# A decode block with a 537 MB key-value cache: 8 MB tiles of 64 KB rows in three slots, K turned in place, scores read in PSUM, 512-wide matmuls, output weights last

## The chip, the core and the metric

The program runs on one core of one Trainium2 chip. The metric is the device time of one execution in microseconds. The median of three executions is 1338.72 us (1338.3 to 1338.79).

## The reference

Two tokens (B = 2 sequences, one position each) pass through one block in float32. The row x (512 wide) is normalized, projected to 32 query heads of 128, and attends to a cache of 8 key-value heads with 32,768 positions each; four query heads share a key-value head. The attention output goes through wo (4096 x 512), and is multiplied by silu of a small gated network of the same x (512 to 1792 to 512).

```python
xn = layernorm(x)
q = (xn @ wq).reshape(2, 1, 32, 128).transpose(0, 2, 1, 3)
scores = einsum("bhqd,bhkd->bhqk", q, repeat(k_cache, 4)) * 128 ** -0.5
p = softmax(scores)
s = einsum("bhqk,bhkd->bhqd", p, repeat(v_cache, 4)).reshape(2, 1, 4096) @ wo
gate, up = xn @ W_gate, xn @ W_up
g = silu(((gate * (gate > 0)) * up) @ W_down)
return x + s * g
```

K and V are 268 MB each. With wq (8.39 MB), wo (8.39 MB), gate and up (7.34 MB) and down (3.67 MB) the core reads 564.67 MB once; nothing of it is used twice.

## The kernel before

**Tiles.** The work falls into 16 groups, one for each pair of sequence and key-value head, each with its 32,768 positions. A group's K and V come in eight tiles each of 4096 positions: 2 MB, in which each of 128 partitions holds 32 consecutive positions, one row of 16 KB. All large loads go through one queue, SP's (`load`, L118), into a ring of eight 16 KB slots per partition, which the weights share. A load is issued when the slot that it takes has been released by its last reader.

**Steps.** The main loop has one step per K tile. `k_transposes` turns the tile on DVE by 32 x 32 blocks, in two instructions of 2048 columns (L282), from its ring slot into one of two further buffers. `scores` (L293) multiplies the turned tile with the group's queries: 16 matmuls of 256 columns, four column groups of the array side by side, and four slices of the head dimension accumulated. One DVE instruction (L303) then scales the scores, copies them from PSUM to SBUF and keeps each row's maximum. When a group's eight tiles are through, `maximum` (L309 to L327) takes the group's maximum through PE and DVE to a negative bias. `weights` runs the exponential on ACT (L333), brings the weights into position with a matmul (L337) and turns them on DVE (L341). `values` multiplies them with a V tile: 32 matmuls of 128 columns in four column groups (L349). At a group's end `take_o` (L369) scales the output by the reciprocal of the sum, and `finish_group` (L377 to L401) brings it into columns. After the second sequence of a head it multiplies with that head's 1 MB of wo (L392) and adds to the sum.

**Order.** The values of a tile come nine steps (`OFF`) behind its scores: in step s the program does the transposes and scores of tile s, the weights of tile s - 8, and the values of tile s - 9. Thus one group's scores run among the values of the group ahead. Loads are written three steps (`DEPTH`) before their use. The gate, up and down weights and the heads' parts of wo are loaded between the K and V tiles. The last V tile comes in three pieces, and behind it the last head's part of wo.

In the trace each matmul of the program appears as two MATMUL and two LDWEIGHTS instructions: 128 tiles with 16 score matmuls give the 4096 of L293.

## Time and profile before

| | |
|---|---|
| median of three executions | 1338.72 us |
| profiled execution: span from first to last instruction | 1336.6 us |
| what the median has beyond that span | 2.1 us |
| busy: PE, DVE, ACT | 847.6, 731.2, 69.1 us |
| mean granted TensorE clock | 0.857 |
| bytes of queue 1 (all loads of SP) | 564.68 MB in 40,776 packets |
| read from HBM | 564.67 MB, 422 GB/s over the span |

Of the profiled execution the profile gives the span alone, and no time of its own. A row of a stage table has the stage, its length, then the busy time and number of instructions of PE, PE's weight loads, DVE, ACT and POOL, then the granted PE clock (1.00 is full), the mean busy share of the 16 DMA engines, and GB/s. A share can pass 1.0 by a little, since packets of one engine overlap at their edges. A row of the groups has line, engine, operation, tiles, shapes and count, then busy us and the mean ns of one, then idle time before them and what ended it. A row of the timeline has start, length, engine, line and count; neighbouring instructions are merged, so its length is that of the whole run.

### The profile page before, as it was taken

What the parts mean: (1) busy time and instruction counts of PE and PEld (TensorE: products, weight loads), DVE (VectorE), ACT (ScalarE), POOL (GpSimd) and SP (SyncE); (2) the same over time, 40 slices, a digit from 0 to 9 for tenths busy, and PEclk for the clock granted to TensorE, in tenths of its full rate; (3) what the DMA queues carried; (4) which work ended last, traced back from release to release, by engine and by line L of the source; (5) the groups of instructions that cost most, each with busy time, mean ns of one, the idle gap of its engine ahead of it and who ended that gap; (6) DMA issues with size and microseconds to landing.
All of it is one profiled execution on the core that took longest, in us unless ns stands there. A gap on an engine that the chain in (4) does not pass through costs nothing.

```text
span 1336.6 us, 28791 instructions
## 1 busy us (share of the span) xinstructions
PE 847.6 (63%) x13288; PEld 487.1 (36%) x13288; DVE 731.2 (55%) x973; ACT 69.1 (5%) x261; POOL 1.3 (0%) x7
## 2 busy tenths in 40 slices
PE   4657666665666656666656666666666666666665
PEld 1333333433334333333434333333333433333343
DVE  5775555646556464555555555465554655556450
ACT  0001010100101010010100001010010100001010
POOL 0000000000000000000000000000000000000000
PEclk9787878978889897888988887898888988789899
DMA  9999999999999999999999999999999999999995
GB/s 397 431 430 430 429 430 429 430 428 430 429 431 428 429 429 430 430 429 428 430 429 430 430 430 430 428 427 431 430 430 430 428 429 428 431 430 424 430 429 246
DMA packets 40951, 566.52 MB, mean 424 GB/s; under 512 B 4462, under 2 KB 4478, under 8 KB 6784
## 3 DMA queue, kind: packets, MB, share of 16 engines
q1 hardware_dynamic: 40776, 564.68, 99.1%
q8 instruction: 104, 1.70, 0.5%
q14 instruction: 15, 0.12, 0.0%
q10 hardware_dynamic: 24, 0.01, 0.0%
q0 software_dynamic: 32, 0.00, 0.0%
HBM read 564.67 MB, written 0.00 MB: 422 GB/s over the span
## 4 chain that ended last, share of the span: by engine, by line
issue 100%; POOLq 0%; POOL 0%
POOLq L488 0%; POOL ident masks.py:199 0%; POOL ident masks.py:197 0%; POOLq masks.py:199 0%; POOLq L475 0%
## 5 line engine op out<-in xcount | busy, mean ns | idle before, releaser
L293 PE MATMUL s<-kts,qt 128*32 128x256 f32 x4096 | 464.7, 523 | 414.9 <-DVE kts L282 409.0
L282 DVE STREAM_TRANSPOSE kts<-k 128x2048 f32<-128x2048 f32 x256 | 573.2, 2277 | 4.2 <-DMA k<-in_A_k_cache_dram 4.2
L293 PEld LDWEIGHTS s<-kts,qt 128*32 128x32 f32 x4096 | 178.1, 140 | 657.7 <-issue 344.8
L349 PE MATMUL o_ps<-v,pts 128*4 128x128 f32 x8192 | 352.4, 297 | 10.0 <-DMA v<-in_A_v_cache_dram 9.5
L349 PEld LDWEIGHTS o_ps<-v,pts 128*4 128x4 f32 x8192 | 260.3, 94 | 71.8 <-issue 21.2
L303 DVE TENSOR_SCALAR_CACHE_REDUCE sc<-s 128x256 f32<-128x256 f32 x128 | 54.3, 425 | 382.5 <-PE s L293 382.4
L341 DVE STREAM_TRANSPOSE pts<-pt 128x256 f32<-128x256 f32 x128 | 57.2, 450 | 143.5 <-PE o_ps L349 129.4
L333 ACT ACTIVATE sc<-sc,nb 128x256 f32<-128x256 f32 x128 | 63.1, 494 | 1143.5 <-DVE nb L327 1143.5
L337 PE MATMUL pt<-sc,perm 128*128 128x256 f32 x256 | 80.0, 415 | 36.2 <-DVE pts L341 32.2
L337 PEld LDWEIGHTS pt<-sc,perm 128*128 128x128 f32 x256 | 39.9, 190 | 62.8 <-issue 42.8
L333 ACT ACTIVATION_READ_ACCUMULATOR sc<-sc,nb 128x1 f32 x128 | 23.8, 186 | 0.0
L369 DVE TENSOR_SCALAR os<-o_ps,rl 128x128 f32<-128x128 f32 x16 | 5.6, 350 | 22.3 <-PE o_ps L349 22.3
L392 PE MATMUL py<-wo,ot 128*32 128x128 f32 x256 | 12.0, 301 | 1.1 <-DMA wo<-in_A_wo_dram 1.1
L187 PE MATMUL pq<-wq,xnt 128*32 128x512 f32 x64 | 10.0, 782 | 1.6 <-DMA wq<-in_A_wq_dram 1.2
L303 DVE DVE_READ_ACCUMULATOR sc<-s 128x1 f32 x128 | 10.7, 83 | 0.0
L392 PEld LDWEIGHTS py<-wo,ot 128*32 128x32 f32 x256 | 8.9, 116 | 1.7 <-DVE ot L387 1.1
L361 DVE TENSOR_REDUCE l<-ls 128x1 f32<-128x8 f32 x16 | 2.5, 158 | 12.5 <-ACT sc L333 12.5
L209 DVE COPY qt<-pqt 32x16 f32<-32x16 f32 x64 | 8.6, 176 | 1.0 <-PE pqt L204 0.6
L175 PE MATMUL px<-ident,boot 32*128 32x32 f32 x4 | 0.9, 287 | 12.5 <-DVE boot L169 12.5
L204 PE MATMUL pqt<-ident,boot 128*128 128x128 f32 x32 | 6.4, 356 | 3.5 <-DVE boot L201 3.5
L231 PE MATMUL ps_g<-wg,xnp 128*32 128x448 f32 x32 | 8.6, 593 | 0.0
L327 DVE COPY nb<-pr 128x1 f32<-128x1 f32 x16 | 2.5, 158 | 9.0 <-PE pr L323 9.0
(70 smaller groups left out, 112.0 us busy)
## 6 DMA issues: line engine op xcount, KB each, us to landing
k<-in_A_k_cache_dram SPq DMA_DIRECT2D x128, 2048.0 KB, 29.4
v<-in_A_v_cache_dram SPq DMA_DIRECT2D x127, 2048.0 KB, 29.5
wq<-in_A_wq_dram SPq DMA_DIRECT2D x4, 2048.0 KB, 13.3
wo<-in_A_wo_dram SPq DMA_DIRECT2D x8, 1024.0 KB, 24.1
wg<-in_B_W_gate_dram SPq DMA_DIRECT2D x2, 1792.0 KB
wu<-in_B_W_up_dram SPq DMA_DIRECT2D x2, 1792.0 KB, 33.5
wd<-in_B_W_down_dram SPq DMA_DIRECT2D x2, 1792.0 KB
v<-in_A_v_cache_dram SPq DMA_DIRECT2D x1, 1024.0 KB
```

What stands on the lines that cost most here:

```text
L187: nc.tensor.matmul(pq[half][32 * c : 32 * c + 32, :], xnt[:, k, :], wqt[k][:, half, c * 512 : (c + 1) * 512], start=(k == 0), stop=(k == N ...
L204: nc.tensor.transpose(pt[:, e, :], rep[:, e].rearrange("p k l -> p (k l)"), ident)
L209: nc.vector.tensor_copy(qt[part, b, half * 4 : half * 4 + 4, :, kb * REP + h], src[:, :, :, b],)
L231: nc.tensor.matmul(ps[32 * c : 32 * c + 32, :FC], xnp[:, k, :], mlp[which, k][:, c * FC : (c + 1) * FC], start=(k == 0), stop=(k == NKC - 1),)
L282: nc.vector.transpose(KTS[t][:, i * half : (i + 1) * half], src[:, i * half : (i + 1) * half])
L293: nc.tensor.matmul(ps[Q * c : Q * c + Q, :], qt[:, b, hk, e, :], mov[:, e, c], start=(e == 0), stop=(e == 3),)
L303: nc.vector.tensor_scalar(ST[t], ps, SCALE, None, op0=ALU.mult, op1=ALU.max, accum_out=MX[g][:, u : u + 1])
L333: nc.scalar.activation(st, st, AF.Exp, bias=NBIAS[g], scale=1.0, accum_out=LS[g][:, u : u + 1])
L337: nc.tensor.matmul(ps, perm.rearrange("p k c h -> p (k c h)"), st, start=True, stop=True)
L341: nc.vector.transpose(PT[t].rearrange("p j m -> p (j m)"), ps)
L349: nc.tensor.matmul(o_ps[Q * a : Q * a + REP, :], w[:, j, c * REP : (c + 1) * REP], v[:, c, j, :], start=(u == 0 and c == 0 and j < 4), sto ...
L392: nc.tensor.matmul(py[32 * c : 32 * c + 32, :P], ot[:, k // 2, k % 2, :], WO[hk][:, k // 2, k % 2, c * P : (c + 1) * P], start=(k == 0), s ...
```

## The change

The tiles become 8 MB: 16,384 positions, 128 in each partition, one row of 64 KB. A group has two K tiles and two V tiles. The ring has three slots of 64 KB per partition, and loads are simply written in the order of their use, K0, K1, V0, V1 of each group, one load per tile. wq takes the first slot, gate and up together the second, down the third; the whole network and the query projection run before the first group.

K is turned in place (L279), eight instructions of 2048 columns per tile, without a second buffer. A tile's scores come in two halves, each 16 matmuls of 512 columns (L282) into a PSUM bank of its own, one bank for each of the group's four halves; DVE only takes the maximum there (L289), and ACT's exponential reads the scores from PSUM and scales them (L316). The values take 32 matmuls of 512 columns per tile (L338): 16 weight columns, those of all four position blocks, against four blocks of V, of which `mask` keeps the fitting quarter in the product with the reciprocal sum (L350). Every second group PE places the outputs (L362) into a bank that gathers all heads. wo is loaded as one 8.39 MB tile in six pieces behind the last V tile, and all 128 output matmuls (L405) come at the end. A group's scores no longer run among another group's values.

In the listing of the change below, `...` and the lines without a sign stand for what is unchanged or left out; the lines that it takes away from these functions are in the listing of the kernel above.

```diff
--- before.py
+++ after.py
-NJ = 8
-NBLK = NC * NJ
-TK = P * NBLK
-LAG = 1
-SLOTS = 8
-DEPTH = 3
+NJ = 16
+ROWS = NS * NC * NJ
+TK = P * ROWS
+SLOTS = 3
 ALIGN = 512
+WO_PIECES = (16, 8, 4, 2, 1, 1)
...
-    ktpool = ctx.enter_context(tc.tile_pool(name="ktpool", bufs=2))
-    spool = ctx.enter_context(tc.tile_pool(name="spool", bufs=NU + LAG + 3))
     work = ctx.enter_context(tc.tile_pool(name="work", bufs=2))
-    ps_s = ctx.enter_context(tc.tile_pool(name="ps_s", bufs=3, space=PSUM))
-    ps_m = ctx.enter_context(tc.tile_pool(name="ps_m", bufs=2, space=PSUM))
-    ps_p = ctx.enter_context(tc.tile_pool(name="ps_p", bufs=2, space=PSUM))
+    ps_c = ctx.enter_context(tc.tile_pool(name="ps_c", bufs=1, space=PSUM))
+
+    SLOT = ROWS * DH
+    KT, VT, PT = {}, {}, {}
+
+    def slot(name):
+        return ring.tile([P, SLOT], F32, tag="r", align_bytes=ALIGN, name=name)
+
+    def load(dst, src):
+        nc.sync.dma_start(dst, src)
+
+    wqs = slot("wq")
+    load(wqs, wq.rearrange("(p i) n -> p (i n)", p=P))
+    wqt = wqs.rearrange("p (i n) -> p i n", i=NKC)
...
+    gus = slot("gu")
+    gut = gus[:, : 2 * NKC * F].rearrange("p (w i f) -> p w i f", w=2, i=NKC)
+    for w, src in enumerate((wg, wu)):
+        load(
+            gus[:, w * NKC * F : (w + 1) * NKC * F],
+            src.rearrange("(p i) f -> p (i f)", p=P),
+        )
+    wds = slot("wd")
+    load(wds[:, : FI * D], wd.rearrange("(p i) d -> p (i d)", p=P))
+    wdt = wds[:, : FI * D].rearrange("p (i d) -> p i d", i=FI)
...
+    S = [[ps_c.tile([P, 512], F32, name=f"s_{u}_{s}") for s in range(NS)] for u in range(NU)]
+    o_ps = ps_c.tile([P, NC, DH], F32, name="o_ps")
+    pt_ps = ps_c.tile([P, 512], F32, name="pt_ps")
+    m_ps = ps_c.tile([P, 512], F32, name="m_ps")
+    ot_ps = ps_c.tile([P, B, NC, Q], F32, name="ot_ps")
...
+    def load_tile(src, t, name):
+        b, hk = group(t // NU)
+        lo = (t % NU) * TK
+        dst = slot(name)
+        load(dst, src[b, hk, lo : lo + TK, :].rearrange("(p r) d -> p (r d)", p=P))
+        return dst
+
+    MX, LS, W, RL, OS = {}, {}, {}, {}, {}
 
     def scores(t):
         g, u = divmod(t, NU)
+        k = KT.pop(t)
         if u == 0:
+            MX[g] = work.tile([P, NU * NS], F32, tag="mx", name=f"mx_{g}")
+        piece = NJ * DH
+        mov = k.rearrange("p (s c j e k) -> p s c e j k", s=NS, c=NC, j=NJ, e=4)
+        for s in range(NS):
+            for c in range(NC):
+                part = slice((s * NC + c) * piece, (s * NC + c + 1) * piece)
+                nc.vector.transpose(k[:, part], k[:, part])
+            for e in range(4):
+                for c in range(NC):
+                    nc.tensor.matmul(
+                        S[u][s][Q * c : Q * c + Q, :],
+                        qt[:, g, e, :],
+                        mov[:, s, c, e],
+                        start=(e == 0),
+                        stop=(e == 3),
+                    )
+            nc.vector.reduce_max(MX[g][:, u * NS + s : u * NS + s + 1], S[u][s], axis=AX.X)
+
+    def soft(g):
         m = work.tile([P, 1], F32, tag="m", name=f"m_{g}")
         nc.vector.reduce_max(m, MX.pop(g), axis=AX.X)
+        nc.tensor.transpose(m_ps[:1, :P], m, ident)
         mr = work.tile([1, REP], F32, tag="mr", name=f"mr_{g}")
         nc.vector.tensor_reduce(
             mr,
+            m_ps[:1, :P].rearrange("o (c k h) -> o h c k", c=4, h=REP)[:, :, :, :4],
             axis=AX.XY,
             op=ALU.max,
         )
+        for c in range(NC):
             nc.vector.tensor_copy(
                 mrow[:, c, :4, :], mr.unsqueeze(1).to_broadcast([1, 4, REP])
             )
         nc.tensor.matmul(
+            m_ps[:, 256:257], mrow.rearrange("o c k h -> o (c k h)"), negs, start=True, stop=True
+        )
+        nb = work.tile([P, 1], F32, tag="nb", name=f"nb_{g}")
+        nc.vector.tensor_copy(nb, m_ps[:, 256:257])
+        LS[g] = work.tile([P, NU * NS], F32, tag="ls", name=f"ls_{g}")
+        for u in range(NU):
+            for s in range(NS):
+                w = work.tile([P, 512], F32, tag="row", name=f"w_{g}_{u}_{s}", bufs=3)
+                i = u * NS + s
+                nc.scalar.activation(
+                    w, S[u][s], AF.Exp, bias=nb, scale=SCALE, accum_out=LS[g][:, i : i + 1]
+                )
+                nc.tensor.matmul(pt_ps, perm[:, s, :], w, start=(s == 0), stop=(s == NS - 1))
+            pt = work.tile([P, NJ, Q], F32, tag="pt", name=f"pt_{g}_{u}")
+            nc.vector.transpose(pt.rearrange("p j m -> p (j m)"), pt_ps)
+            PT[g * NU + u] = pt
+        l = work.tile([P, 1], F32, tag="l", name=f"l_{g}")
+        nc.vector.reduce_sum(l, LS.pop(g), axis=AX.X)
         nc.tensor.matmul(
+            m_ps[:, 300:301], same.rearrange("p r h -> p (r h)"), l, start=True, stop=True
+        )
+        RL[g] = work.tile([P, 1], F32, tag="rl", name=f"rl_{g}")
+        nc.vector.reciprocal(RL[g], m_ps[:, 300:301])
 
     def values(t):
+        u = t % NU
+        v = VT.pop(t).rearrange("p (s c j d) -> p s j c d", s=NS, c=NC, j=NJ)
+        w = PT.pop(t)
+        for s in range(NS):
             for j in range(NJ):
                 a = j % 4
                 nc.tensor.matmul(
+                    o_ps[Q * a : Q * a + NC * REP],
+                    w[:, j, s * NC * REP : (s + 1) * NC * REP],
+                    v[:, s, j],
+                    start=(u == 0 and s == 0 and j < 4),
+                    stop=(u == NU - 1 and s == NS - 1 and j >= NJ - 4),
+                )
 
     def finish_group(g):
         b, hk = group(g)
+        if b == 0:
+            OS[hk] = work.tile([P, B, NC, DH], F32, tag="os", name=f"os_{hk}", bufs=1)
+        nc.vector.scalar_tensor_tensor(
+            OS[hk][:, b],
+            o_ps,
+            RL.pop(g),
+            mask.unsqueeze(2).to_broadcast([P, NC, DH]),
+            op0=ALU.mult,
+            op1=ALU.mult,
+        )
+        if b == B - 1:
+            src = OS.pop(hk).rearrange("p b c (q i) -> p q (b c) i", q=4)
+            for dq in range(4):
+                lo = P - 4 * REP * hk - dq
                 nc.tensor.matmul(
+                    ot_ps.rearrange("p b c i -> p (b c) i"),
+                    place[:, lo : lo + P],
+                    src[:, dq],
+                    start=(hk == 0 and dq == 0),
+                    stop=(hk == HKV - 1 and dq == 3),
+                )
+
     project_q()
...
+    for g in range(NG):
+        for u in range(NU):
+            KT[g * NU + u] = load_tile(kc, g * NU + u, f"k_{g}_{u}")
+        for u in range(NU):
+            VT[g * NU + u] = load_tile(vc, g * NU + u, f"v_{g}_{u}")
+        for u in range(NU):
+            scores(g * NU + u)
+        soft(g)
+        if g % 3 == 2 and g // 3 < 4:
+            c = g // 3
+            nc.scalar.dma_start(xy[32 * c : 32 * c + B, :], x[:, 0, c * P : (c + 1) * P])
+        for u in range(NU):
+            values(g * NU + u)
+        finish_group(g)
+
+    wos = slot("wo")
+    worows = wo.rearrange("(p i) d -> p (i d)", p=P)
+    i = 0
+    for n in WO_PIECES:
+        load(wos[:, i * D : (i + n) * D], worows[:, i * D : (i + n) * D])
+        i += n
+    for b in range(B):
+        nc.vector.tensor_reduce(
+            ot[:, :, b], ot_ps[:, b].rearrange("p c i -> p i c"), axis=AX.X, op=ALU.add
+        )
+    py = S[0][0]
+    wot = wos.rearrange("p (i d) -> p i d", i=WI)
+    for i in range(WI):
+        for c in range(4):
+            nc.tensor.matmul(
+                py[32 * c : 32 * c + B, :P],
+                ot[:, i, :],
+                wot[:, i, c * P : (c + 1) * P],
+                start=(i == 0),
+                stop=(i == WI - 1),
+            )
+    nc.vector.tensor_mul(res, py[:, :P], gy)
+    nc.vector.tensor_add(res, res, xy)
+    for b, eng in enumerate((nc.sync, nc.scalar)):
+        eng.dma_start(
+            out[b, 0, :].rearrange("(c n) -> c n", c=4),
+            res.rearrange("(c m) n -> m c n", c=4)[b],
+        )
```

Two places show how instructions move. First DVE at the border of two groups. Before (`os`: the finished group's output; `pts`: turned weights; `kts`: turned K; `sc`: scores):

```order
L327 COPY nb_1162<-pr_1153 128x1
L369 TENSOR_SCALAR os_1208<-o_ps,rl_1174 128x128
L341 STREAM_TRANSPOSE pts_1168<-pt_1166 128x256
L387 COPY ot<-po_1210 64x4 x2
L341 STREAM_TRANSPOSE pts_1246<-pt_1244 128x256
L341 STREAM_TRANSPOSE pts_1309<-pt_1307 128x256
L361 TENSOR_REDUCE l_1706<-ls_1164 128x1
L282 STREAM_TRANSPOSE kts_1128<-k_1000 128x2048 x2
L303 TENSOR_SCALAR sc_1149,mx_1148<-s_1131 128x256
L341 STREAM_TRANSPOSE pts_1372<-pt_1370 128x256
```

Here a turned K tile and one tile's turned weights alternate, and the next group's scores are already done when a group's output is scaled. The same place in the changed kernel:

```order
L310 COPY nb_406<-m_ps 128x1
L321 STREAM_TRANSPOSE pt_0_415<-pt_ps 128x512
L324 TENSOR_REDUCE l_425<-ls_408 128x1
L321 STREAM_TRANSPOSE pt_1_423<-pt_ps 128x512
L329 RECIPROCAL rl_428<-m_ps 128x1
L350 SCALAR_TENSOR_TENSOR os_494<-o_ps,rl_428,mask 128x512
L279 STREAM_TRANSPOSE k_0_496<-k_0_496 128x2048 x6
L289 TENSOR_REDUCE mx_504<-s_0_117 128x1
L279 STREAM_TRANSPOSE k_0_496<-k_0_496 128x2048 x2
L289 TENSOR_REDUCE mx_504<-s_1_118 128x1
```

The product with the reciprocal sum (L350), which needs all values of the group, now stands ahead of all K transposes of the next group, and the maximum of a first half stands between the transposes of the second.

Second, the end of PE's program in the changed kernel (`v_0`, `v_1`: the last two V tiles; `ot_ps`: the gathered outputs; `s_0_117`: the bank that now takes the result):

```order
L325 MATMUL m_ps<-l_3345,same 128x1
L338 MATMUL o_ps<-v_0_3227,pt_0_3335 16x512 x32
L338 MATMUL o_ps<-v_1_3229,pt_1_3343 16x512 x32
L362 MATMUL ot_ps<-os_3221,place 128x256 x4
L405 MATMUL s_0_117<-wo,ot 2x128 x128
```

All output matmuls moved behind the last group; before, only the last head's 16 stood there.

More of the change, by code (lines that the diff above doesn't have):

```diff
@@ L179 @@
-    nc.vector.tensor_copy(xnt.rearrange("p k m -> p (k m)"), px[:, : NKC * 32])
-    nc.vector.tensor_copy(xnp.rearrange("p k m -> p (k m)"), px[:, NKC * 32 : 2 * NKC * 32])
-    def project_q():
-        pq = [ps_m.tile([P, 512], F32, tag="m", name=f"pq_{half}") for half in range(2)]
-        for k in range(NKC):
-            for half in range(2):
+    xcol = xc.rearrange("b (p i) -> b i p", i=NKC)
+    for i in range(NKC):
+        nc.tensor.transpose(m_ps[:, i * 32 : (i + 1) * 32], xcol[:, i, :], ident[:32, :32])
@@ new lines @@
+    nc.vector.tensor_copy(xnp.rearrange("p k m -> p (k m)"), m_ps[:, : NKC * 32])
+    def project_q():
+        pick = ident.rearrange("p (c m) -> p c m", c=4)[:, :, :B]
+        nq = 2 * REP * 4 * B
+        spread = work.tile([P, 4, 4, Q], F32, tag="row", name="spread", bufs=3)
+        for kb in range(4):
+            nc.vector.tensor_copy(
+                spread[:, :, kb, :], ident.rearrange("p (e l) -> p e l", e=4)
+            )
+        for half in range(2):
+            pq = S[0][half]
+            for i in range(NKC):
@@ L215 @@
[L215 to L229 removed]
+                lo = (half * REP + h) * 4 * B
@@ L247, in mlp_h @@
         nc.vector.tensor_mul(g[:, :FC], g[:, :FC], u[:, :FC])
-        ht = const.tile([P, FI, 32], F32, name="ht")
+        ht = work.tile([P, FI, 32], F32, tag="row", name="ht", bufs=3)
         nc.vector.transpose(
@@ L273, in mlp_down, with group @@
                 )
-        nc.scalar.activation(gy, ps[:, :P], AF.Silu)
-    def k_transposes(t):
-        src = KT.pop(t).rearrange("p c j d -> p (c j d)")
-        KTS[t] = ktpool.tile([P, NBLK * DH], F32, tag="kt", name=f"kts_{t}")
-        half = NBLK * DH // 2
-        for i in range(2):
-            nc.vector.transpose(
-                KTS[t][:, i * half : (i + 1) * half], src[:, i * half : (i + 1) * half]
-            )
+        nc.scalar.activation(gy, m_ps[:, :P], AF.Silu)
+    def group(g):
+        return g % B, g // B
@@ L318, in maximum @@
         )
-        for c in range(4):
+        for c in range(NC):
             nc.vector.tensor_copy(
@@ L347, in values @@
+        v = VT.pop(t).rearrange("p (s c j d) -> p s j c d", s=NS, c=NC, j=NJ)
+        w = PT.pop(t)
+        for s in range(NS):
             for j in range(NJ):
@@ L349, in values @@
                 nc.tensor.matmul(
-                    o_ps[Q * a : Q * a + REP, :],
-                    w[:, j, c * REP : (c + 1) * REP],
-                    v[:, c, j, :],
-                    start=(u == 0 and c == 0 and j < 4),
-                    stop=(u == NU - 1 and c == NC - 1 and j >= 4),
-                )
-    OS, RL = {}, {}
-    def sums(g):
-        l = work.tile([P, 1], F32, tag="l", name=f"l_{g}")
-        nc.vector.reduce_sum(l, LS.pop(g), axis=AX.X)
-        pr = ps_m.tile([P, 512], F32, tag="m", name=f"pl_{g}")
-        nc.tensor.matmul(pr[:, :1], same.rearrange("p r h -> p (r h)"), l, start=True, stop=True)
-        RL[g] = work.tile([P, 1], F32, tag="rl", name=f"rl_{g}")
-        nc.vector.reciprocal(RL[g], pr[:, :1])
```

337 lines of the change are left out of this document (89 added, 248 removed).

## The prediction

> **What bounds the kernel now.** I read the page first: engines, the DMA line and the DMA queues.
>
> ```profile
> span 1336.6 us, 28791 instructions
> PE 847.6 (63%) x13288; PEld 487.1 (36%) x13288; DVE 731.2 (55%) x973; ACT 69.1 (5%) x261; POOL 1.3 (0%) x7
> PEclk9787878978889897888988887898888988789899
> DMA  9999999999999999999999999999999999999995
> q1 hardware_dynamic: 40776, 564.68, 99.1%
> q8 instruction: 104, 1.70, 0.5%
> ```
>
> No compute engine is busy for two thirds of the span; the 16 DMA engines are, from end to end. So the time is 564.68 MB through them, plus a head and a tail. Then I read the stages of both ends (the last two columns are DMA share and GB/s).
>
> ```profile
> 0.00:2.00 2.00, 0.00 (x0) 0.00 (x0) 0.94 (x6) 0.00 (x0) 0.70 (x6) 1.00 0.51 98
> 2.00:4.00 2.00, 0.00 (x0) 0.00 (x0) 1.79 (x2) 0.51 (x1) 0.00 (x0) 1.00 0.61 197
> 100.00:1300.00 1200.00, 771.04 (x12228) 445.95 (x12226) 661.18 (x801) 64.64 (x256) 0.00 (x0) 0.86 1.01 429
> 1308.00:1312.00 4.00, 2.60 (x66) 1.91 (x66) 0.39 (x2) 0.00 (x0) 0.00 (x0) 1.00 1.04 433
> 1312.00:1316.00 4.00, 1.42 (x53) 1.40 (x57) 0.16 (x1) 0.00 (x0) 0.00 (x0) 1.00 0.78 330
> 1316.00:1320.00 4.00, 1.02 (x40) 0.69 (x32) 0.45 (x1) 0.00 (x0) 0.00 (x0) 0.99 0.57 240
> 1324.00:1328.00 4.00, 3.00 (x97) 2.47 (x99) 0.00 (x0) 0.00 (x0) 0.00 (x0) 1.00 0.50 207
> 1330.00:1332.00 2.00, 0.55 (x13) 0.49 (x17) 0.67 (x3) 0.00 (x0) 0.00 (x0) 1.00 0.25 102
> ```
>
> The start loses 4.0 - 2 x (98 + 197)/430 = 2.6 us. At the end the share halves: a share of 0.78 over four microseconds means that half of the engines stop at 1314.2, and 0.25 over two that the others stop at 1331.0. Eight engines lag by 16.8 us, and the program ends with them. The likeliest cause is the instruction queue: its 1.70 MB over PE's 26,576 instructions (13,288 matmuls, as many weight loads) are 64 bytes each, in 104 packets. On eight engines that is 13 each; 0.5% of 16 x 1336.6 us is 107 us of engine time, 13 us on each of eight, near the lag; 1.3 us a packet with what surrounds it. The fast half carried its bytes at 564.68 MB/(1314.2 - 2.6) = 430.5 GB/s for all sixteen.
>
> **The change: the stream.** The bytes stay the same. Per group 33.55 MB arrive, which takes 77.9 us, and one 8.39 MB tile 19.5 us.
> (1) PE instructions. In the trace a matmul of the program counts twice. After: scores 32 tiles x 32 x 2 = 2048, values 2048, turning weights 128, output weights 256, the four projections some 240, the new placing 64, small ones 100: about 4,890, with weight loads 9,780, or 38 packets. The lag becomes 16.8 x 38/104 = 6.2 us: 10.6 us gained. If the lag is not from instructions, nothing.
> (2) Rows of 64 KB, and 75 loads where there were about 275. No row shows such a packet. At the end eight engines moving 8 and 4 KB rows reach 207 GB/s, where half of 430.5 is 215: 3.8%, or 8 ns a row of some 5.5 KB. If all of that is a cost per row, 64 KB rows save three quarters of 8 ns in each 16 KB row's 609 ns, 13 us over the stream. Below, zero. Instruction packets lie in that window too, so I take 5.
> All bytes then land at 1314.2 + 6.2 - 5 = 1315.4. The last 8.39 MB are the output weights, so the last V tile lands at 1295.9. The first K tile lands behind 27.8 MB, at 2.6 + 64.6 = 67.2.
>
> **The change: one chain per group.** Before, scores of one group ran among the values of another. Now DVE's product o x 1/l (L350 of the new kernel) waits for the last V tile's matmuls, and behind it on DVE stand the next group's K transposes, for which PE's scores wait; transposes, scores, maximum, weights and values of a group stand in one line. This line is new work for the bound: it must fit in 77.9 us. Its terms:
>
> ```profile
> L282 DVE STREAM_TRANSPOSE kts<-k 128x2048 f32<-128x2048 f32 x256 | 573.2, 2277 | 4.2 <-DMA k<-in_A_k_cache_dram 4.2
> L341 DVE STREAM_TRANSPOSE pts<-pt 128x256 f32<-128x256 f32 x128 | 57.2, 450 | 143.5 <-PE o_ps L349 129.4
> L333 ACT ACTIVATE sc<-sc,nb 128x256 f32<-128x256 f32 x128 | 63.1, 494 | 1143.5 <-DVE nb L327 1143.5
> L196 DVE COPY qs<-pq 128x512 f32<-128x512 f32 x2 | 1.4, 688 | 10.2 <-PE pq L187 10.2
> ```
>
> Transposes in place have the old shape: 573.2/256 = 2.24 us each, sixteen a group as before. A 512-wide PSUM reduction is unseen; between 0.43 (256 wide) and twice that, I take the 512-wide copy's 0.69. Matmuls, from the timeline:
>
> ```profile
> 23.13 1.92 PE L187 MATMUL pq<-wq,xnt 128*32 128x512 f32 x16 [1.18 <-DMA wq<-in_A_wq_dram]
> 797.30 0.63 PE L293 MATMUL s<-kts,qt 128*32 128x256 f32 x4 [1.11 <-DVE kts L282]
> 799.41 1.71 PE L293 MATMUL s<-kts,qt 128*32 128x256 f32 x26 [1.48 <-DVE kts L282]
> 811.93 0.42 DVE L303 TENSOR_SCALAR_CACHE_REDUCE sc<-s 128x256 f32<-128x256 f32 x1 [3.29 <-PE s L293]
> 814.37 0.51 ACT L333 ACTIVATE sc<-sc,nb 128x256 f32<-128x256 f32 x1 [78.16 <-DVE nb L327]
> 815.99 1.13 PE L337 MATMUL pt<-sc,perm 128*128 128x256 f32 x4
> 823.07 3.20 PE L293 MATMUL s<-kts,qt 128*32 128x256 f32 x26 [1.48 <-DVE kts L282]
> 832.16 1.06 PE L293 MATMUL s<-kts,qt 128*32 128x256 f32 x4 [1.52 <-DVE kts L282]
> 1302.46 1.93 PE L349 MATMUL o_ps<-v,pts 128*4 128x128 f32 x64
> ```
>
> Four 512-wide passes side by side take (1.92 - 0.2)/4 = 0.43 us; so half a K tile's scores take 8 x 0.43 = 3.45 us and end 0.2 later, and a V tile 16 x 0.43 = 6.9 where 64-pass pieces took 4 x 1.93 = 7.7. The same 26 matmuls take 1.71 us in one place and 3.20 in another: the clock granted there is full or half.
> K tile at full clock: eight transposes 17.9, two reductions 1.4, the second half's scores 3.65 (the first half's hide under transposes five and six), 0.1 of hand-over: 23.0. Maximum to first exponential 2.0 (811.93 + 0.42 to 814.37). Two 512-wide exponentials, 1.5 (unseen; between 0.49 and twice that I take 0.76, longer by what the 512-wide copy takes over the 256-wide reduction); turned through PE 1.0 and DVE 0.9 (twice 0.45); the second pair through PE 2.0; row sums 0.4. Values 13.9. Product 0.75. Together 46.0 + 2.0 + 5.8 + 14.65 = 68.5 us.
> Clock: 24.6 us of it are matmuls. At the 0.86 of the middle window they grow by 4.0; with a half clock the first half's scores end 2.6 us after transpose six, in say a third of the tiles, 1.8. So 74 to 75; I take 75, bounds 68.5 and, all at half clock, 98. It fits, by 3 us.
>
> A page speaks against this. The Trainium skill, TensorE: Matmul & The Clock Gate, section Why this matters for your kernels, says that one idle window between bursts, some 3 us, drops the clock to half. The trace agrees in the two prices of 26 matmuls. By that rule K's scores would run mostly at half clock and the chain would be near 84.
>
> I keep 75, since the score matmuls of the first three pieces (0.63 us for four at full clock, 1.06 at half; 512 wide up to twice that) fill nearly half of each 2.24 us between transposes, at half clock most of it, and the middle window ran at 0.86 with the same transposes.
>
> Three slots: a tile must be free two tile times, 39 us, after landing. K0 is free after 22, K1 26 after its own landing, V0 and V1 25 and 16. None is late, so the stream isn't held up. A load that waits for its slot holds all later loads behind it on SP, but these need slots that come free later still.
>
> **The tail** grows: all output weights need the last group.
>
> ```profile
> 1331.87 1.08 PE L392 MATMUL py<-wo,ot 128*32 128x128 f32 x32 [1.06 <-DMA wo<-in_A_wo_dram]
> 1333.33 0.29 DVE L404 TENSOR_TENSOR res<-res,base 128x128 f32<-128x128 f32 x1
> 1333.65 0.65 SPq L461 DMA_DIRECT2D out_dram<-res  x2
> ```
>
> The last group's first K tile lands 58.5 before 1295.9, at 1237.4; its chain ends at 1312.4. Placing, eight 256-wide passes at 1.13/4: 2.3; two reductions of 128 columns 0.6; 256 output passes like L349's 64 in 1.93: 7.7; hand-overs 0.3; the matmuls end at 1323.3. The weights landed at 1315.4, so they are hidden. From the last matmul before (1332.95) to the span's end are 3.65. **Sum:** 1327.0, 9.6 under the span; the median lies 2.1 above this span (1338.72), so 1329.
>
> **Rivals.**
> A, the other side: the chain outlasts the stream. The place is DVE's queue, product ahead of transposes; the price is the half clock, 1.49 us for each 26 matmuls in the rows above. The end is then 67.2 + 16 x chain + 14.6: chain 78.5 gives 1338 (1340 as median, no change; the point from which it decides), 80 gives 1362 (1364). With all scores at half clock, 2 x (2.6 + 3.45) = 12.1 more and some 3 at the values' start, it is 84: 1426. For: 3 us of room in 75. Against: slots absorb some 7 us before the stream stops, and the clock row shows 0.7 to 0.9 throughout. 0.20.
> B, the lag isn't the instruction packets and stays: 10.6 us later, 1337.6, median 1340: same. Against: 104 is 8 x 13. 0.09.
> C, the full clock holds: chain 68.5 ends at 1306, the output matmuls end behind the weights at 1316.7: 1320.4, median 1322.5. 0.06.
> D, rows 64 KB apart are read more slowly. At the lowest rate seen, 2 x 207 = 414 GB/s, 556 MB take 50 us more: 1379. For: nothing but that such rows are unseen. Against: 16 KB rows give 429 throughout. 0.05.
>
> **Numbers.** My forecast, 0.60: 1329, its own range 1323 to 1336 (row saving 0 to 13, chain 73 to 77). Faster by over 0.2% (below 1336; about what a measurement here can tell): 0.60 + C 0.06 = 0.66. Same: B 0.09 and A's edge near 78.5, 0.02: 0.11. Slower: the rest of A 0.18, and D 0.05: 0.23. The range 1321 to 1350 holds the forecast, B, C and A up to a chain of 79.
>
> **What would show it.** After: PE near 4,900 matmuls, queue 8 near 38 packets; the time from 0.5 to zero DMA share near 6 us; GB/s 431 or more in the middle; the product's end under 78 us after the group's first K transpose, and K's first transpose waiting for DMA, not for PE. A DMA share under 0.98 in the middle, or K transposes that begin with no wait for DMA, prove A; a lag of 17 us proves B; a full share at under 425 GB/s D.

## The result, and the profile after

The changed kernel takes 1320.86 us (median of four times, 1319.81 to 1321.2; the kernel before 1338.61 beside it): a ratio of 0.9866, 95% interval 0.9852 to 0.988. Faster, then, as forecast, but by 17.8 us where 9.6 were forecast: 8 us under the predicted 1329, and just under the range, which began at 1321. The profiled execution has a span of 1318.0. First its page:

```profile
span 1318.0 us, 10841 instructions
PE 874.6 (66%) x4892; PEld 216.5 (16%) x4892; DVE 674.1 (51%) x569; ACT 49.0 (4%) x133; POOL 0.7 (0%) x6
PEclk9779788888988878878887967889788877989789
q1 hardware_dynamic: 10664, 564.66, 99.0%
q8 instruction: 38, 0.62, 0.2%
```

The bytes are the same, in a quarter of the packets, and 38 packets of instructions are left of 104. The stages of both ends (last three columns: granted clock, DMA share, GB/s):

```profile
0.00:2.00 2.00, 0.00 (x0) 0.00 (x0) 1.10 (x4) 0.00 (x0) 0.70 (x6) 1.00 1.19 393
2.00:4.00 2.00, 0.00 (x0) 0.00 (x0) 1.62 (x5) 0.73 (x1) 0.00 (x0) 1.00 0.37 131
100.00:1280.00 1180.00, 800.13 (x4148) 186.38 (x4148) 625.65 (x486) 41.82 (x120) 0.00 (x0) 0.84 1.00 434
1302.00:1304.00 2.00, 1.55 (x16) 0.23 (x8) 0.39 (x1) 0.00 (x0) 0.00 (x0) 1.00 0.92 379
1304.00:1308.00 4.00, 3.00 (x48) 2.41 (x51) 0.85 (x3) 0.00 (x0) 0.00 (x0) 1.00 0.54 226
1308.00:1310.00 2.00, 2.00 (x84) 1.94 (x76) 0.00 (x0) 0.00 (x0) 0.00 (x0) 1.00 0.42 160
1310.00:1312.00 2.00, 2.00 (x76) 1.64 (x69) 0.00 (x0) 0.00 (x0) 0.00 (x0) 1.00 0.06 22
```

The head loses 4.0 - 2 x (393 + 131)/434 = 1.6 us (2.6 before). A share of 0.92 over 1302 to 1304 puts the stop of the fast half at 1303.7; 0.42 and then 0.06 put that of the slow half at 1309.9. So the lag is 6.2 us (16.8 before), the fast half stops 10.5 us earlier than before (1314.2), and the slow half 21.1 earlier (1331.0).

The groups' chains stand in the waits of DVE (total, times, longest) and in the timeline:

```profile
DVE mx L289 <- PE s L282: 161.9, 33, 6.5
DVE k L279 <- DMA k<-in_A_k_cache_dram: 121.1, 16, 22.3
```

```profile
68.63 4.50 DVE L279 STREAM_TRANSPOSE k<-k 128x2048 f32<-128x2048 f32 x2 [22.26 <-DMA k<-in_A_k_cache_dram]
...
1233.36 4.50 DVE L279 STREAM_TRANSPOSE k<-k 128x2048 f32<-128x2048 f32 x2 [7.51 <-DMA k<-in_A_k_cache_dram]
...
1303.62 0.75 DVE L350 SCALAR_TENSOR_TENSOR os<-o_ps,rl,mask 128x512 f32<-128x512 f32 x1 [13.23 <-PE o_ps L338]
...
1307.00 7.43 PE L405 MATMUL s<-wo,ot 128*2 128x128 f32 x256 [0.58 <-DVE ot L398]
```

K's transposes wait for DMA 16 times: 22.3 us ahead of the first group, and 98.8 together ahead of the other fifteen, 6.6 each. From the first transpose (68.63) to the last product's end (1304.37) sixteen chains take 1235.7 - 98.8 = 1136.9, or 71.1 each. Of the 64 reductions 33 wait for scores, 161.9 us in all: the 32 that belong to the second half of a tile, and one more by 0.15. Most of that wait is there at any clock: in the last experiment below, which keeps the clock up, each of the 32 waits 3.71 us (the prediction had 3.65), 118.7 together. The other 43 us, 2.7 a group, are the clock. The last chain ends at 1304.37, and the program 13.6 us later.

### The profile page after: what moved, and what is told of

Read it like the earlier page. It is cut to its first block, busy times and chain, and to the rows that moved or that the text cites. A ratio compares the mean times of both kernels' runs of the same rounds, so it can differ in the third digit from the quotient of the medians.

```text
span 1318.0 us, 10841 instructions
## 1 busy us (share of the span) xinstructions
PE 874.6 (66%) x4892; PEld 216.5 (16%) x4892; DVE 674.1 (51%) x569; ACT 49.0 (4%) x133; POOL 0.7 (0%) x6
## 3 DMA queue, kind: packets, MB, share of 16 engines
q1 hardware_dynamic: 10664, 564.66, 99.0%
## 4 chain that ended last, share of the span: by engine, by line
DVE 44%; DMA 39%; PE 16%; issue 1%; ACT 0%; ACTq 0%; DVEq 0%
DVE k L279 42%; DMA k<-in_A_k_cache_dram 37%; PE s L282 13%; DMA wq<-in_A_wq_dram 2%; DVE mx L289 2%; PE o_ps L338 1%; PE s L178 1%; PE s L405 1%; PE pt_ps L319 0%; PE ot_ps L362 0%; DVE os L350 0%; DVE pt L321 0%; DVE ot L398 0%; DVE mrow L303 0%; PE m_ps L306 0%
## 5 line engine op out<-in xcount | busy, mean ns | idle before, releaser
L282 PE MATMUL s<-k,qt 128*32 128x512 f32 x2048 | 517.7, 735 | 343.0 <-DVE k L279 342.8
L279 DVE STREAM_TRANSPOSE k<-k 128x2048 f32<-128x2048 f32 x256 | 568.3, 2277 | 121.1 <-DMA k<-in_A_k_cache_dram 121.1
L338 PE MATMUL o_ps<-v,pt 128*16 128x512 f32 x2048 | 224.6, 596 | 0.0
L282 PEld LDWEIGHTS s<-k,qt 128*32 128x32 f32 x2048 | 91.3, 127 | 765.3 <-DVE k L279 609.4
L289 DVE TENSOR_REDUCE mx<-s 128x1 f32<-128x512 f32 x64 | 43.2, 675 | 162.0 <-PE s L282 161.9
L350 DVE SCALAR_TENSOR_TENSOR os<-o_ps,rl,mask 128x512 f32<-128x512 f32 x16 | 12.0, 751 | 214.0 <-PE o_ps L338 214.0
L319 PE MATMUL pt_ps<-w,perm 128*128 128x512 f32 x128 | 72.0, 690 | 32.3 <-ACT w L316 17.9
L316 ACT ACTIVATE w<-s,nb 128x512 f32<-128x512 f32 x64 | 43.1, 686 | 1185.6 <-DVE nb L310 1185.6
L338 PEld LDWEIGHTS o_ps<-v,pt 128*16 128x16 f32 x2048 | 57.2, 97 | 152.9 <-issue 152.7
L321 DVE STREAM_TRANSPOSE pt<-pt_ps 128x512 f32<-128x512 f32 x32 | 22.9, 717 | 89.7 <-PE pt_ps L319 89.7
L319 PEld LDWEIGHTS pt_ps<-w,perm 128*128 128x128 f32 x128 | 23.6, 205 | 65.9 <-ACT w L316 45.6
L362 PE MATMUL ot_ps<-os,place 128*128 128x256 f32 x64 | 16.0, 392 | 7.0 <-DVE os L350 7.0
L362 PEld LDWEIGHTS ot_ps<-os,place 128*128 128x128 f32 x64 | 11.5, 189 | 15.6 <-DVE os L350 14.4
L316 ACT ACTIVATION_READ_ACCUMULATOR w<-s,nb 128x1 f32 x64 | 12.9, 202 | 0.0
```

Source lines behind the costliest of these rows:

```text
L279: nc.vector.transpose(k[:, part], k[:, part])
L282: nc.tensor.matmul(S[u][s][Q * c : Q * c + Q, :], qt[:, g, e, :], mov[:, s, c, e], start=(e == 0), stop=(e == 3),)
L289: nc.vector.reduce_max(MX[g][:, u * NS + s : u * NS + s + 1], S[u][s], axis=AX.X)
L316: nc.scalar.activation(w, S[u][s], AF.Exp, bias=nb, scale=SCALE, accum_out=LS[g][:, i : i + 1])
L319: nc.tensor.matmul(pt_ps, perm[:, s, :], w, start=(s == 0), stop=(s == NS - 1))
L321: nc.vector.transpose(pt.rearrange("p j m -> p (j m)"), pt_ps)
```

## The experiments

Two theories had to share the gain: fewer instruction packets (a smaller lag), and a cheaper stream (rows of 64 KB). A third question was how near the chain is to the bound.

**The lag: the loads alone.** All computation is left out; one column of each tile is copied, so that its slot comes free.

```diff
+    def touch(t, width):
+        i = n_seen[0]
+        n_seen[0] += 1
+        nc.vector.tensor_copy(seen[:, i % 128 : i % 128 + 1], t[:, width - 1 : width])
-    ... (all projections, scores, values and products)
```

> Only the loads of the changed kernel: the same bytes in rows of 64 KB through three slots, each released by a copy of one column on DVE; all computation is left out, and PE has no instructions. Theory P (eight DMA engines lag because they fetch PE's instructions too): both halves of the engines end together, within 1 us, at about 1303, and the span is 1306-1308; queue 8 has hardly a packet. Rival B (the lag belongs to the data or to the engines): a lag of 5 us or more between the halves, span 1312 or more.

Measured: span 1307.2, time 1309.0. The end, by windows (DVE, POOL, then clock, DMA share, GB/s):

```profile
1302.00:1303.00 1.00, 0.00 (x0) 0.00 (x0) 1.00 1.02 397
1303.00:1304.00 1.00, 0.00 (x0) 0.00 (x0) 1.00 0.45 172
1304.00:1305.00 1.00, 0.15 (x1) 0.00 (x0) 1.00 0.03 10
```

There is no stage of half share: all engines stop at about 1303.5, where the changed kernel's fast half does (1303.7). So the rest of that kernel, its clock and its chains, costs the fast half 0.2 us at most.

**The lag: the loads and idle matmuls.**

```diff
+N_PE = 98
...
+        for j in range(N_PE):
+            nc.tensor.matmul(
+                spare[:, j : j + 1], zero, seen[:, i % 128 : i % 128 + 1], start=True, stop=True
+            )
```

> The run with the loads alone, and 98 matmuls of one column behind each of the 68 tiles (into a tile that nobody reads), 6,664 in all, four PE instructions each: 26,656 instructions, as many as the kernel before the change has, and hardly any PE time. Theory P: 104 packets of queue 8, 13 on each of eight engines, and these end 13 x 1.3 = 16.8 us behind the others: DMA share 0.5 from about 1303 to 1320, span 1322-1325. Rival B: the same end as the run with the loads alone, within 2 us.

Measured: the estimate of PE's time was far off: with 128 columns of weights these matmuls take 2,843 us, the span is 2867.2, and fewer than half of the packets fall into the stream. The end of its stream (PE, PEld, DVE, POOL, clock, DMA share, GB/s):

```profile
1304.00:1306.00 2.00, 2.00 (x11) 2.00 (x11) 0.00 (x0) 0.00 (x0) 1.00 0.53 224
1310.00:1312.00 2.00, 2.00 (x11) 2.00 (x11) 0.00 (x0) 0.00 (x0) 1.00 0.47 185
1312.00:1314.00 2.00, 2.00 (x11) 2.00 (x11) 0.15 (x1) 0.00 (x0) 1.00 0.04 14
```

Half share from about 1304 to 1312: the 8 us of some 48 packets. Two columns of weights mend it:

```diff
-                spare[:, j : j + 1], zero, seen[:, i % 128 : i % 128 + 1], start=True, stop=True
+                spare[:2, j : j + 1], zero[:, :2], seen[:, i % 128 : i % 128 + 1], start=True, stop=True
```

> The run with the loads alone and 6,664 matmuls of one column, but with two columns of weights each instead of 128, so that PE keeps up with the loads: with 128 columns PE took 2,843 us, twice the stream, and only some 48 of the 104 packets were fetched while it ran (the halves of the DMA engines then ended 8 us apart, 6 x 1.3). Theory P: now all 104 packets come in the stream, 13 on each of eight engines: half share of DMA from about 1304 to 1320-1321, span about 1324. Rival B (the lag isn't proportional to the packets): the same 8 us as there, or less.

Measured, queue 8 first and then the windows (PE, PEld, DVE, POOL, clock, DMA share, GB/s):

```profile
q8 instruction: 104, 1.70, 0.5%
```

```profile
1302.00:1304.00 2.00, 0.32 (x13) 0.32 (x14) 0.15 (x1) 0.00 (x0) 1.00 0.92 378
1304.00:1306.00 2.00, 2.00 (x86) 2.00 (x83) 0.00 (x0) 0.00 (x0) 1.00 0.46 200
...
1320.00:1322.00 2.00, 0.00 (x0) 0.00 (x0) 0.00 (x0) 0.00 (x0) 1.00 0.42 166
1322.00:1324.00 2.00, 0.92 (x37) 0.93 (x38) 0.15 (x1) 0.00 (x0) 1.00 0.04 14
```

The fast half stops at 1303.7, the slow half at 1321.7: 18.0 us for 13 packets on each of its engines, 1.4 us a packet. With the packets of the kernel before, its lag is back, with no other work. (The span, 1329.0, ends with the last tile's idle matmuls, not with a byte.) That PE works isn't the cause: in the run before, PE was busy 99% of the time, and the lag was about half as long, with about half of the packets in the stream. Theory P is shown.

**Rows: four loads by columns.** Each row of 64 KB becomes four of 16 KB, in four loads.

```diff
-        load(dst, src[...].rearrange("(p r) d -> p (r d)", p=P))
+        rows = src[...].rearrange("(p r) d -> p (r d)", p=P)
+        for i in range(4):
+            part = slice(i * SLOT // 4, (i + 1) * SLOT // 4)
+            load(dst[:, part], rows[:, part])
```

> The changed kernel with each load of an 8.39 MB K or V tile cut into four loads by columns: 128 rows of 16 KB each, into the same slot and in the same order. Slots, instructions of PE, DVE and ACT, and bytes stay; packets go from 10,664 to about 35,000 and loads from 75 to about 267. Theory R (the fast half of the DMA engines stops at about 1304 instead of 1314 because a row of 64 KB has a quarter of the fixed costs of four rows of 16 KB): the middle goes back from 434 to 430-431 GB/s and all ends 7 to 9 us later, 1328-1330 as median, ratio to the kernel before 0.992-0.993. Theory N (the cost is one per load, for its completion): the same 7 to 9 us here, told apart from R by the run with quarters of partitions. Rival M (the gain of the middle is from fewer instruction packets alone): within 1.5 us of the changed kernel, 1320-1322.

Measured: 1325.33 us (1325.19 to 1325.54), ratio 0.9903 (0.9888 to 0.9918).

```profile
100.00:1280.00 1180.00, 828.34 (x4119) 189.89 (x4118) 622.50 (x483) 42.20 (x120) 0.00 (x0) 0.82 1.01 431
1316.00:1318.00 2.00, 1.72 (x60) 1.15 (x48) 0.00 (x0) 0.00 (x0) 0.00 (x0) 1.00 0.46 181
1318.00:1320.00 2.00, 1.44 (x36) 0.53 (x32) 0.21 (x1) 0.00 (x0) 0.00 (x0) 1.00 0.20 73
```

The middle falls from 434 to 431 and the bytes end at 1318.8, 8.9 us later, as both R and N said. The end moves by 4.5 only: transposes now begin on a quarter of a tile (the first at 54.3 instead of 68.6), the chains run ahead, and the bytes take over the end from the last chain. M falls; rows and loads aren't told apart yet.

**Loads: four loads by partitions.** `rows` is the same as in the run before.

```diff
+        for i in range(4):
+            part = slice(i * P // 4, (i + 1) * P // 4)
+            load(dst[part], rows[part])
```

> The changed kernel with each load of a K or V tile cut into four loads by partitions: 32 rows of 64 KB each. Rows keep 64 KB, so packets stay at some 10,700 to 13,700 (with the packets that report a load done), but loads go from 75 to about 267. Theory R (cost per row): 0 to 2 us later than the changed kernel, 1321-1323. Theory N (cost per load): as the run with rows of 16 KB, 1328-1330. Rival M: 1320-1322, as R, and then the run with rows of 16 KB stands there too.

Measured: 2660.62 us, twice the time. None of the theories had this; the DMA engines are busy throughout at half the rate:

```profile
100.00:2600.00 2500.00, 926.38 (x4276) 210.66 (x4278) 650.39 (x508) 45.63 (x128) 0.00 (x0) 0.67 1.00 209
```

The Trainium skill, SBUF — State Buffer, section "Door 1: The DMA port swizzle (why `[64,N]` ≈ `[32,N]`)", says that partitions 0 to 31 reach 8 of 16 ports, some 218 GB/s. The 209 GB/s agree. By its table, every fourth partition would reach all 16. The next two runs separate rows and loads without this trap.

**Rows of 16 KB in one load; and four loads spread over all partitions.**

```diff
# the first: 75 loads, 512 rows of 16 KB each
+        load(
+            dst.rearrange("p (i f) -> p i f", i=4),
+            src[...].rearrange("(i p r) d -> p i (r d)", i=4, p=P),
+        )
# the second: some 267 loads, 32 rows of 64 KB each
+        for i in range(4):
+            load(dst[i::4], rows[i::4])
```

> The changed kernel with each K and V tile still brought by one load, of 512 rows of 16 KB in place of 128 rows of 64 KB: partition p takes four stretches of keys from four places of the cache (K and V alike, so the sums over keys are the same sums in another order). Packets as in the run with four loads by columns (some 35,000), loads as in the changed kernel (75), nothing waits for a quarter of a tile. In the run with four loads by columns the middle moved 431 GB/s and all bytes were there some 9 us later, with the end 4.5 us later, since in the changed kernel the last chain ends 4 us behind the bytes. Theory R (the cost is one per row of 16 KB): again 431 GB/s, half share of DMA until about 1319, end 1325-1326 as median. Theory N (one per load): 434 GB/s and 1320-1322.

> The changed kernel with each K and V tile in four loads of 32 rows of 64 KB, load i to partitions i, i+4, i+8 and so on. It takes the place of the run with four loads to 32 neighbouring partitions each, in which a packet of 64 KB took twice its time and the stream ran at 209 GB/s. Theory Q (32 neighbouring partitions are filled at half the rate, whatever the number of loads): spread over all partitions the full rate is back, so that load counts can be compared: by R (a cost per row) 434 GB/s and 1321-1323, by N (a cost per load) 431 GB/s and 1325-1326. Rival (a load of 32 rows is slow in itself): near 2660 again.

Measured: rows of 16 KB in one load 1330.7 us (1327.18 to 1333.87; ratio 0.9942, 0.9922 to 0.9962); four spread loads 1320.75 (1318.21 to 1323.61; ratio 0.9875, 0.9858 to 0.9891). The middle of the first and its last group:

```profile
100.00:1280.00 1180.00, 823.54 (x4124) 190.49 (x4123) 625.04 (x486) 42.09 (x120) 0.00 (x0) 0.82 1.01 431
```

```profile
1240.49 4.50 DVE L282 STREAM_TRANSPOSE k<-k 128x2048 f32<-128x2048 f32 x2 [1.46 <-DMA k<-in_A_k_cache_dram]
...
1313.42 0.75 DVE L353 SCALAR_TENSOR_TENSOR os<-o_ps,rl,mask 128x512 f32<-128x512 f32 x1 [13.74 <-PE o_ps L341]
```

And the middle and the end of the second:

```profile
100.00:1280.00 1180.00, 818.39 (x4151) 191.84 (x4149) 627.32 (x487) 42.26 (x120) 0.00 (x0) 0.83 1.00 433
1308.00:1310.00 2.00, 2.00 (x84) 1.93 (x76) 0.00 (x0) 0.00 (x0) 0.00 (x0) 1.00 0.53 216
1310.00:1312.00 2.00, 2.00 (x83) 1.93 (x76) 0.00 (x0) 0.00 (x0) 0.00 (x0) 1.00 0.28 107
```

R stands: 75 loads of small rows run at 431, 267 loads of long rows at 433. The number of loads costs little: 192 loads more bring 3,072 small packets more (13,736 in all), and the bytes end at 1311.1, where the changed kernel has 1309.9 and, in its second profile (the run `again` below), 1310.2. With 16 KB rows the last group's first K tile is there at 1240.5 instead of 1233.4 (1233.7 in the second profile): 7.1 us by then, or 7.5 scaled to the whole stream, for 35,240 - 10,664 = 24,576 packets more: 16 x 7.5/24,576 = 4.9 ns of an engine for each. My end for it (1325 to 1326) was 5 us too early: I carried over the slack of the run by columns, which comes from transposing quarters of a tile. Without it, the later landing goes through the last chain in full, and that chain took 73.7 us here against 71.0: 7.1 + 2.7 = 9.8, and the two spans (1327.7 and 1318.0) are 9.7 apart.

**The chain: two or eight more transposes a group.** The piece is turned three times, which gives the same tile.

```diff
                 nc.vector.transpose(k[:, part], k[:, part])
+                if u == 0 and s == 0 and c == 0:      # eight more: if c == 0
+                    nc.vector.transpose(k[:, part], k[:, part])
+                    nc.vector.transpose(k[:, part], k[:, part])
```

> The changed kernel in which one piece of each group's first K tile is turned three times instead of once in each of the 16 groups (the same result, two more transposes on DVE, 2 x 2.24 = 4.5 us per group). Theory S (the chain of a group, 71 us, fits in the 77.4 us that its 33.55 MB take to arrive, and only the last group's chain shows): the chain grows to 75.6, still under 77.4, and the end moves by the last group's 4.5 us alone: 1325-1326. Rival A (the chain sets the pace already, and the waits for DMA only fill what is left): 16 x 4.5 = 72 us, near 1392. Rival D (the loads set the end and the tail hides 4.5 us): unchanged, 1321.

> The changed kernel in which one piece of each half of a K tile is turned three times (four such places a group: eight more transposes, 8 x 2.24 = 17.9 us per group; the same result). Theory S: the chain is 71 + 17.9 = 89 us, longer than the 77.4 us of a group's bytes; from there the chain sets the pace: first K tile at about 67 + 16 x 89 + 13.4 = 1504 as span, DMA share near 0.87 in the middle, and K's first transpose waiting for the product of the group before instead of DMA. Rival L (groups overlap by more than the chain of waits shows, so that DVE's own 42 us a group are the bound): only the last group's 17.9 us, near 1336.

Measured: two more, 1321.57 us (1320.05 to 1329.73; ratio 0.9892, 0.9858 to 0.9927); eight more, 1447.29, with a span of 1445.5. The first, by its groups and its last product:

```profile
L279 DVE STREAM_TRANSPOSE k<-k 128x2048 f32<-128x2048 f32 x256 | 570.9, 2278 | 58.4 <-DMA k<-in_A_k_cache_dram 58.4
```

```profile
1303.41 0.75 DVE L353 SCALAR_TENSOR_TENSOR os<-o_ps,rl,mask 128x512 f32<-128x512 f32 x1 [13.23 <-PE o_ps L341]
```

The waits for DMA shrink from 121.1 to 58.4, so the mean chain is 75.0, 3.9 longer, sixteen times; and the end stays. Rival A falls: the stream sets the pace, though with little room left. Single chains pass 77 us (up to 80.3), three begin without a wait for DMA, and the fast half of the DMA engines stops at 1309.6 instead of 1303.7.

My theory S had the end 4.5 us later, by the last group's two transposes. That number failed, and rival D's (unchanged) was met, but not for its reason: the output matmuls end at 1315.6, 4 us behind the last byte (1311.5). The last chain itself is no longer than before, 69.8 us against 71.0. Its second reduction, in the changed kernel and here, shows one part of why:

```profile
1247.13 4.49 DVE L279 STREAM_TRANSPOSE k<-k 128x2048 f32<-128x2048 f32 x2
1257.03 0.69 DVE L289 TENSOR_REDUCE mx<-s 128x1 f32<-128x512 f32 x1 [5.41 <-PE s L282]
```

```profile
1252.51 6.67 DVE L279 STREAM_TRANSPOSE k<-k 128x2048 f32<-128x2048 f32 x3
1260.70 0.69 DVE L292 TENSOR_REDUCE mx<-s 128x1 f32<-128x512 f32 x1 [1.52 <-PE s L285]
```

In the program as built the edit also moved a transpose: the second K tile's first one now stands ahead of this reduction and fills 2.2 us of its wait. The clock gave the other part: the last group's two reductions wait 1.52 + 3.71 us instead of twice 5.41, 5.6 less, of which 2.2 are the transpose and 3.4 the clock, against 4.4 of added work. The clock's part is luck, as far as these runs show: in other groups of this trace the second of these waits is up to 6.6, and the longest of the four times is 8 us over the median.

With eight more, DVE's waits and the ends of the row of chains:

```profile
DVE mx L292 <- PE s L285: 92.4, 46, 4.3
DVE k L279 <- DMA k<-in_A_k_cache_dram: 22.3, 1, 22.3
```

```profile
68.70 4.50 DVE L279 STREAM_TRANSPOSE k<-k 128x2048 f32<-128x2048 f32 x2 [22.26 <-DMA k<-in_A_k_cache_dram]
...
1431.27 0.75 DVE L353 SCALAR_TENSOR_TENSOR os<-o_ps,rl,mask 128x512 f32<-128x512 f32 x1 [13.23 <-PE o_ps L341]
```

Only the first group waits for DMA: the chain is the bound, and the stream waits for slots. It is (1432.0 - 68.7)/16 = 85.2 us in the mean, not 89, since the reductions wait 92.4 us instead of 161.9, 4.3 less a group: 71.1 + 17.9 - 4.3 = 84.7. Again the order moved as well: two transposes of the second K tile (4.4 us) now stand ahead of the first tile's last reduction. The clock isn't the reason, with 0.796 against 0.847.

**The tail: another order of the last two groups.** In the changed kernel the output matmuls end at 1314.4, behind the last chain and 4.5 us behind the last byte of their weights. Here `a` is group 14's first tile and `z` group 15's; the listing joins several lines into one.

```diff
-    for g in range(NG):
+    for g in range(NG - 2):
...
+    load_k(a); load_k(a + 1); load_v(a); load_k(z); load_v(a + 1)
+    scores(a); scores(a + 1); soft(NG - 2); values(a)
+    load_k(z + 1); scores(z); values(a + 1); finish_group(NG - 2)
+    load_v(z); load_v(z + 1)
+    scores(z + 1); soft(NG - 1); values(z); values(z + 1); finish_group(NG - 1)
```

> The changed kernel with the last two groups in another order of loads: K0 and K1 of group 14, its V0, then K0 of group 15, V1 of group 14, K1, V0 and V1 of group 15, and group 15's first K tile scored between the two V tiles of group 14. The work is the same. In the changed kernel the last chain ends at 1304.4, after that come 2.6 us of placing and 7.4 us of output matmuls to 1314.4, while the output weights are there at 1310.3. Theory S (the chain of the last group sets the end, by 4 us over the landing of the weights): the last chain then begins with one K tile instead of two behind it, the output matmuls end just after the last piece of the weights, at about 1310.8, and the span is 1314-1315: 3 to 4 us faster, median 1317-1318. Rival D (the bytes set the end already): no change, 1321. Rival: the other order makes a slot late, and the stream stops for it: slower, 1325 or more.

> The changed kernel itself once more, beside the run with the other order of the last two groups: 1320-1322.

Measured side by side: the other order 1317.03 us (1316.92 to 1319.22; ratio to before 0.984, 0.9826 to 0.9853), the changed kernel once more 1320.41 (1318.74 to 1322.67; 0.9866, 0.9853 to 0.988). The 3.4 us are what was expected, though the intervals touch. It is the fastest version here, beside the next one. The bytes are the same, so they alone didn't set the changed kernel's end. Its last K tile and last product, from an execution with a span of 1317.4 (the other four have 1315.1 to 1315.4):

```profile
1253.00 13.28 DVE L279 STREAM_TRANSPOSE k<-k 128x2048 f32<-128x2048 f32 x6 [8.74 <-DMA k<-in_A_k_cache_dram]
...
1301.71 0.75 DVE L350 SCALAR_TENSOR_TENSOR os<-o_ps,rl,mask 128x512 f32<-128x512 f32 x1 [13.80 <-PE o_ps L338]
```

From the one to the other's end are 49.5 us.

**The clock: the other order, with the first matmuls of a piece done twice.**

```diff
                 nc.vector.transpose(k[:, part], k[:, part])
+                spare = [pt_ps[Q * c : Q * c + Q, :]] if c < NC - 1 else []
+                for to in [S[u][s][Q * c : Q * c + Q, :]] + spare:
+                    nc.tensor.matmul(
+                        to, qt[:, g, 0, :], mov[:, s, c, 0], start=True, stop=bool(spare) and to is spare[0]
+                    )
-            for e in range(4):
+            for e in range(1, 4):
...
-                        start=(e == 0),
+                        start=False,
```

> The run with the other order of the last two groups, and behind the first score matmul of each of the first three pieces of a half tile the same matmul once more into a bank that is free then (nobody reads it): 192 matmuls more, some 3 more instruction packets. In the changed kernel one such matmul takes 1.04 us at full clock of the 2.24 between two transposes, so PE is busy 46% there, and K's reductions wait 161.9 us for scores in 33 places; chains run from 68.2 to 73.8 us, mean 71.1, in the run with the other order 49.5 us from the last K tile's first transpose to the last product. Theory H (chains over 68.2 us lose the rest to a PE clock that falls while PE idles between transposes): filled to 90%, the clock stays up, all full groups are at 68-69 us, reductions wait under 120 us, the last K tile to the last product takes 45-46 us, and the median is 1314-1316. Rival (the second matmul holds up the real ones, or the waits are not the clock): chains as before or longer, 1317 or more.

Measured: 1317.69 us (1316.77 to 1318.9; ratio 0.9845, 0.9832 to 0.9858), the same as without. Its span is 1315.9. The waits of the reductions (total, times, longest), first with the other order alone and then here, and the end here:

```profile
DVE mx L289 <- PE s L282: 179.2, 42, 6.7
DVE mx L294 <- PE s L287: 118.8, 32, 3.7
```

```profile
1252.85 13.28 DVE L279 STREAM_TRANSPOSE k<-k 128x2048 f32<-128x2048 f32 x6 [9.09 <-DMA k<-in_A_k_cache_dram]
...
1300.03 0.75 DVE L355 SCALAR_TENSOR_TENSOR os<-o_ps,rl,mask 128x512 f32<-128x512 f32 x1 [13.23 <-PE o_ps L343]
...
1303.41 4.64 PE L438 MATMUL s<-wo,ot 128*2 128x128 f32 x161 [0.58 <-DVE ot L431]
1309.44 2.80 PE L438 MATMUL s<-wo,ot 128*2 128x128 f32 x95 [1.39 <-issue]
```

The mechanism is there. The granted clock is 0.894 where the other order alone had 0.829 and the changed kernel 0.847. Exactly the 32 second-half reductions wait, each 3.71 us: 118.8 instead of 179.2 in all (161.9 in the changed kernel). All fourteen full chains lie between 67.6 and 70.5, mean 69.1, where the other order alone has 68.2 to 78.0, mean 73.9, and the changed kernel 68.2 to 73.8. From the last K tile to the last product it is 47.9 us, 1.6 less than without, and not the 3.5 to 4.5 that I expected: the two waits for the turned weights in that group are 4.14 and 3.79 us, where the changed kernel's last group has 2.95 and 2.10, and there nothing fills PE.

But no time comes of it, so the median is where the rival had it. The last bytes land at about 1310.5 in this trace, and the output matmuls can't end before them. They end at 1312.2, behind a pause of 1.4 us with no wait that the profile shows, and 3.6 us more follow. A pause of 1.2 us stands at the same place in the other order alone and in the second profile of the changed kernel. Its cause is open, and with it what the shorter chain would be worth without it.

## Why the prediction was right in kind and wrong in size

By its own steps, against the profiled span (1327.0 forecast, 1318.0 measured):

**The bound** held: DMA at full share from end to end, the rest behind it.

**(1) PE instructions** held in every number: 4,892 matmuls (forecast 4,890), 38 packets (38), a lag of 6.2 us (6.2). That packets make the lag was an inference from one sum; the loads with and without idle matmuls show it.

**(2) Rows of 64 KB is one of the two steps that failed.** I took 5 out of 0 to 13, some 3 ns a row. The runs show 4.9 ns, 7.5 us for the rows of K and V. The kernel before had 40,776 packets, 5,536 more than the run with rows of 16 KB; at the same 4.9 ns these are some 1.7 us (an estimate). The head gave 1.0 that I hadn't counted. Together 10.2, of the 10.5 by which the fast half stops earlier. So all bytes landed at 1309.9, not 1315.4. For the rows of K and V the truth lay midway between what I took and the upper bound; the fewer small packets and the head, which I had at nothing, gave the rest.

**The chain's clock is the other.** The chain was 71.1 us where I took 75. The terms at full clock held (68.5; the trace's shortest chains have 68.2), but the clock cost 2.6 us, not the 6.5 that I added. Of my two terms for it, the 1.8 for the first half's scores came to nothing (of the 32 first-half reductions one waits, 0.15 us): PE is done with them before the transposes of the next half's first two pieces end. The 4.0 for slower matmuls came to 2.7, in the second half's scores (43 us of waits beyond the full clock); I had spread it over all matmuls, but the wait for the values' matmuls is 13.4 in the mean and 13.2 at its least. Rounding up to 75 added the rest. What makes one chain lose more than another is open, and the wait ahead of it doesn't tell: in the second profile of the changed kernel a chain that begins without a wait takes 75.2 us, one behind a wait of 10.4 us 68.2. The chains of that profile are 71.7 in the mean, but reach 78.0, as long as the 77.9 that the forecast gave a group's bytes.

**The tail** from product to end took 13.6, not 14.6 (output matmuls 7.4, not 7.7; placing 2.0, not 2.3; the rest less by little). No slot was late (DMA share 1.00 in the middle).

**The sum**: the last group's first K tile came 4.0 us earlier than I had it (1233.4 for 1237.4; the bytes were 5.5 earlier, but a group's transposes begin later than I had the landing, 68.6 for 67.2 in the first group), its chain was 4.0 shorter (71.0 for 75), the tail 1.0: 9.0. The times lie 2.9 over this span where I had allowed 2.1: 8.1 under the forecast. Two terms erred to the same side, each by 4 us. The low end missed it because neither 1323 nor C's 1322.5 puts both terms at their good end: C has the short chain beside a row saving of 5, and the forecast's own bounds taken together (saving 13, chain 73) give 1329 - 8 - 2 = 1319 by the same sum.

**The rivals.** A didn't come, but its mechanism is real: with eight more transposes the chain passes 77 us and sets the end. B is refuted by the loads alone. C came about halfway: five of the sixteen chains are as short as it had them, 68.2 to 68.4. D is refuted: long rows are the faster ones. **The rule of the Trainium skill** (TensorE: Matmul & The Clock Gate, section Why this matters for your kernels: an idle window drops the clock to half; by it the chain would be 84) came in part: 26 of the 32 second-half reductions wait longer than the 3.71 us of the full clock, but the longest wait is 6.5, under the 7.2 that half clock throughout would give (an estimate, 3.71 + 3.45). The row of the middle window, 0.86 before and 0.84 after, was the better guide.

## What to carry to other kernels

When DMA is the bound, count packets of all kinds: the data's (here some 5 ns for each) and the instructions', which here half of the DMA engines carry and which the last byte waits for. So fewer and wider matmuls shortened a kernel whose PE was never the bound. And bound a sum's terms jointly: two unknown terms that may both be at their good end make a range's end together. When an experiment adds instructions, look at the order in the new trace: here it moved others too.
